# A fused attention and gated-MLP kernel: the row sums of one weight matrix split over two stages, output weights loaded later, transposes interleaved

## The chip, the cores and the metric

The kernel runs on one core of a Trainium2 chip. The metric is the time of one execution on the device in microseconds (us), lower is better. A core has TensorE (matmuls), VectorE, ScalarE and GpSimd, SyncE (SP) that mostly issues transfers, and 16 DMA engines that move data between device memory (DRAM) and the on-chip SBUF. Each engine works through its own instructions in order and waits on semaphores for others.

## The reference

Inputs are bf16; S = 2048 tokens, D = 1024, 32 heads of 32, FH = 1792.

```python
# A: sliding dilated attention; window of 8, dilation 2
qkv = layernorm(x) @ wqkv            # per token and head: softmax over k at s, s-2, ..., s-14
h = x + attn @ wo
# B: gated MLP with a spatial (token by token) mix
z = gelu(layernorm(h) @ w_in)        # [S, 2*FH]
z1, z2 = z[:, :FH], layernorm(z[:, FH:])
g = w_sp @ z2 + b_sp[:, None]        # w_sp is [S, S]
out = h + (z1 * g) @ w_out
```

## The kernel before, in words

Tokens are cut into four chunks of 512 (`NCH`), each of four tiles of 128 (`TPC`). Three stages follow each other.

**Attention and projections, chunk by chunk.** `qkv` multiplies the normed chunk with the weights; ScalarE copies each result out of PSUM (L461 into the tiles of chunk 0, L466 into a staging tile that SP stores to `qkv_d`). `attention` works on VectorE: products of q and k (L513), sums, then the scores go through TensorE (L543), a maximum, ScalarE's exp (L564) and a reciprocal. Half of the weights reach all partitions by way of DRAM: SP stores `att_d` and loads it back into `AB` (L592), and VectorE's products with v for the last four window places (L629) wait for it. GpSimd issues two accumulating DMAs for the first four. The result `oT` goes to `head` (L700: times wo, plus the residual, a layernorm, and an SP transpose into `hnT`; the last chunk has one transpose for each tile). Then `b_z2` (L777) and `b_z1` (L831) multiply with w_in; the gelu is ScalarE's; `z2` gets its second layernorm (the `l3` values, L808 on VectorE for the last chunk) and both are stored to DRAM. In the last chunk ScalarE issues these stores itself.

The order on TensorE, ScalarE, VectorE and GpSimd is written out by a planner (`Order`): each step has an engine, an assumed cost in us, its predecessors and a priority, and the planner runs through the steps in assumed time. Steps of kind `DMA` with a cost stand for transfers or for plain delays. The engines' instructions are then issued in that order; on the chip only semaphores decide the times. From `close_` on SP's order is by hand too.

**Row sums of w_sp.** The weight matrix w_sp is scaled per row by a power of two, so that its products fit fp16. For that `wsp_sums` loads its 16 row tiles (`wn`, 512 KB each, from ScalarE's DMA queue, four buffers) and ScalarE adds up absolute values in two halves of each (L859). `row_scales` turns the 16 columns into scales on VectorE; they are turned on TensorE, stored (`rs_d`) and loaded on all partitions (`rows`). In the planner the loads start at 45 us and follow every 8 us.

**The spatial stage.** w_sp is loaded transposed by SP (`load_raw`: chunks 0 and 1 as rawa and rawb before the stage, 2 and 3 within it), multiplied by `rows` (`scale_raw`, L897), and combined into three forms (`t_forms`). The product with z2 is done by seven half-size products in place of eight for each block (L1011), for each of two pairs of chunks (`pr`) and seven pairs of feature tiles (`i`; `n = 7 pr + i`). For one n, TensorE runs k1, k4, k3, k2 (8 matmuls each), then second products into k1, k4 and k3 (8 each). Before those ScalarE must have copied k1 to p1, k4 to p7 and k3 to p5 (L1047, L1049, L1051). VectorE forms the sums of z2 for the next n (`z_form`, tiles `zs`), then combines the results with p1, p7, p5 (L1065 to L1075), and GpSimd helps (L1056 to L1071). z2f and z1c are loaded two and one n ahead by SP.

**The output projection** follows each pair of chunks: eight row tiles (`il`), 28 matmuls each (L1092), with VectorE's residual (L1095) and, in the first pair, the scaling and the forms of chunks 2 and 3. Its weights `wout_a` and `wout_b` are loaded by GpSimd's queue as soon as the planner's part is written out.

Of the kernel before, what the change touches and what calls it, by code (L numbers as in the profile page):

```python
# [24 lines left out]
CH = 512  # L25
NCH = S // CH
TPC = CH // P
KT = D // P
DLO = 8
HALO = 16  # L30
# [10 lines left out]
L2DVE = (0, 0, 2)  # L41
PIECES = ((0, 0), (0, 4), (1, 0), (1, 4))
LNPRIO = (0, 2.0, 2.5, 2.8)
WSP_FROM, WSP_EVERY = 45.0, 8.0
HK = S // P // 2
LAST_COLS = ((0, 512), (512, 896), (896, 1024))

# [83 lines left out]
def kernel(  # L131
# [260 lines left out]
    def dma_op(us, fn, deps, lat=0.1, free=None):  # L392
        return add("DMA", us, fn, deps, lat=lat, free=free)
# [453 lines left out]

    def wsp_sums():
        tl = {}
        for i in range(NT):  # L850
            def ld(i=i):
                tl[i] = l1.tile([P, S], BF16, name="wn", tag="x4k", bufs=4)
                A.dma_start(tl[i][:], B_w_sp[i * P:(i + 1) * P, :])
            gate = add("DMA", WSP_FROM + WSP_EVERY * i, lambda: None)
            l_ = dma_op(4.0, ld, [gate, wabs_ops[i - 4] if i >= 4 else G["normed", 2]])
            for hf in range(2):
                def ab(i=i, hf=hf):
                    h_ = tl[i][:, hf * D:(hf + 1) * D]
                    A.activation(h_, h_, ACTF.Abs, accum_out=wabs[:, i, hf:hf + 1])  # L859
                a_ = add("ACT", 1.22, ab, [l_], prio=5.8)  # L860
            wabs_ops.append(a_)

    def row_scales():
        V.tensor_tensor(wlim[:], wabs[:, :, 0], wabs[:, :, 1], op=ALU.add)
        V.tensor_scalar(wlim[:], wlim[:], 2.0 ** -40, 2.0 ** 60, op0=ALU.max, op1=ALU.min)
        V.tensor_scalar(wexp[:], wlim[:].bitcast(I32), 0x7F800000, None, op0=ALU.bitwise_and)
        V.tensor_scalar(rsc[:], wexp[:], -1.0, float(266 << 23), op0=ALU.mult, op1=ALU.add)
        V.tensor_scalar(rinv[:], wexp[:], float(-(12 << 23)), None, op0=ALU.add)
        V.tensor_copy(rsc16[:], rsc[:].bitcast(FP32))

    def rows_turned():
        wt_["ps"] = ps_acc.tile([P, 2, 2 * CH], BF16, name="rps", tag="acc")
        T.transpose(wt_["ps"][0:NT, 0, 0:P], rsc16[:], ident[:])

    def rows_out():
        A.copy(rscT[0:NT, :], wt_["ps"][0:NT, 0, 0:P])
        dma(rs_d[:], rscT[0:NT, :])

    def rows_in():
        wt_["rows"] = zpools["z"].tile([P, S], BF16, name="rows")  # L880
        dma(wt_["rows"][:], rs_d[:].rearrange("i p -> (i p)").unsqueeze(0).to_broadcast([P, S]))

    def bias_rows(pr, pool, tag, bufs):
        cols = slice(2 * pr * CH, (2 * pr + 2) * CH)
# [30 lines left out]
    def load_z2f(n, hf):  # L915
        if hf == 0:
            z2f[n] = zpools["z"].tile([P, NT, 2 * P], BF16, name="z2f", tag="z2f", bufs=2)
        i = n % (NF // 2)
        dma(z2f[n][:, hf * HK:(hf + 1) * HK, :], z2_view[:, hf * HK:(hf + 1) * HK, 2 * i * P:(2 * i + 2) * P])
# [44 lines left out]
        zpools["z"] = ctx.enter_context(tc.tile_pool(name="zpool", bufs=1, side="right"))  # L964

    head(NCH - 1)
    rs_ = add("DVE", 1.0, row_scales, [G["avdone", NCH - 1]] + wabs_ops, prio=2.8)
    rt_ = add("PE", 0.1, rows_turned, [rs_], prio=0.5, take="acc", lat=0.2)
    ro_ = add("ACT", 0.3, rows_out, [rt_], prio=1.0, free="acc")
    rl_ = dma_op(4.0, rows_in, [(ro_, 2.5), G["close"]])  # L970
    b_z2(NCH - 1)
    b_z1(NCH - 1)
    r0_ = dma_op(9.0, lambda: load_raw(0), [G["hnT", NCH - 1]])
    r1_ = dma_op(9.0, lambda: load_raw(1), [r0_])
    prev = []
    for c, r_ in ((0, r0_), (1, r1_)):
# [5 lines left out]
    z_ld = {}  # L982
    for n in range(2):
        for hf in range(2):
            z_ld[n, hf] = dma_op(4.0, lambda n=n, hf=hf: load_z2f(n, hf), [r1_] + [G["z2st", 2 * hf + c, il] for c in range(2) for il in range(TPC)])
    prev = None
    for m in (3, 1, 2, 4):
        prev = add("DVE", 0.7, lambda m=m: z_form(0, m), [z_ld[0, 0]] + ([z_ld[0, 1]] if m != 3 else []) + ([prev] if prev else []), prio=3.0)
    o_.run()
    wout_a = wtile([P, 8, D], "wout_a", "wA")  # L990
    wout_b = wtile([P, NF - 8, D], "wout_b", "wA")
    wout_view = B_w_out.rearrange("(f p) n -> p f n", p=P)
    dma_w(wout_a[:], wout_view[:, 0:8, :])
    dma_w(wout_b[:], wout_view[:, 8:NF, :])
    t2.close()
    bph_stack.close()
    ps_stack.close()
# [29 lines left out]
    for pr in range(NCH // 2):  # L1027
# [5 lines left out]
        for i in range(NQ):  # L1033
            n = pr * NQ + i
            z = z2f[n]
            a11, a12, a22 = z[:, 0:HK, 0:P], z[:, HK:NT, 0:P], z[:, HK:NT, P:2 * P]
            p1, p7, p5, u = f32("p1"), f32("p7"), f32("p5"), f32("u2")
            if n == 0:
                load_z1c(0)
            if n + 1 < 2 * NQ:  # L1040
                load_z1c(n + 1)
            if i == 0:
                zg = p2.tile([P, NF, 2 * CH], BF16, name="zg", tag="zg", bufs=1)
            z1c = z1cs[n]
            k1, k4, k3, k2 = bank(), bank(), bank(), bank()
            times(k1, a11, b11, True)
            A.copy(p1[:], k1[:])  # L1047
            times(k4, zs[n, 3], t3, True)
            A.copy(p7[:], k4[:])  # L1049
            times(k3, zs[n, 1], t1_, True)  # L1050
            A.copy(p5[:], k3[:])  # L1051
            times(k2, zs[n, 2], t2_, True)
            times(k1, a12, b21, False)
            times(k4, a22, t4_, False)
            times(k3, zs[n, 4], b22, False)
            nc.gpsimd.tensor_tensor(p7[:], p7[:], p5[:], op=ALU.add)  # L1056
            if pr == 0 and i < TPC:
                load_raw(2, i, i + 1)
            if i + 1 < NQ:
                for m in (3, 1, 2, 4):  # L1060
                    z_form(n + 1, m)
            if n + 2 < 2 * NQ:
                for hf in range(2):
                    load_z2f(n + 2, hf)
            V.tensor_tensor(u[:], k2[:], p1[:], op=ALU.add)  # L1065
            nc.gpsimd.tensor_tensor(p1[:], u[:], bt1, op=ALU.add)
            nc.gpsimd.tensor_tensor(u[:], u[:], bt2, op=ALU.add)
            z11, z12 = zg[:, 2 * i, 0:CH], zg[:, 2 * i, CH:2 * CH]
            z21, z22 = zg[:, 2 * i + 1, 0:CH], zg[:, 2 * i + 1, CH:2 * CH]
            V.tensor_tensor(z11, k1[:], bt1, op=ALU.add)  # L1070
            nc.gpsimd.tensor_tensor(z22, p7[:], u[:], op=ALU.add)  # L1071
            V.tensor_tensor(z21, k4[:], p1[:], op=ALU.add)
            V.tensor_tensor(zg[:, 2 * i + 1, :], zg[:, 2 * i + 1, :], z1c[:, 1, :], op=ALU.mult)
            V.tensor_tensor(z12, k3[:], u[:], op=ALU.add)
            V.tensor_tensor(zg[:, 2 * i, :], zg[:, 2 * i, :], z1c[:, 0, :], op=ALU.mult)  # L1075
            if pr == 0 and i > TPC:
                scale_raw(2, (i - TPC - 1) * HK)
            if i == NQ - 2:
                for il in range(3):
                    load_hr(2 * pr * TPC + il)  # L1080
        for il in range(2 * TPC):
# [28 lines left out]
                    finish_(lo, hi, acc)  # L1110
                    (A.dma_start if n % 2 else dma)(out2d[t * P:(t + 1) * P, lo:hi], hr[:, lo:hi])
            if pr == 0:
                if il == 3:
                    scale_raw(3, 0)
                    scale_raw(3, HK)
                elif il == 4:
# [41 lines left out]
```

## Time and profile before

| | |
|---|---|
| median of 3 runs | 742.01 us (741.72 to 742.41) |
| the profiled execution | 742.02 us, its span 740.0 us |
| mean granted TensorE clock | 0.979 |
| busy: TensorE, VectorE, ScalarE, GpSimd | 95%, 68%, 37%, 16% |
| DMA | 133 MB, 180 GB/s in the mean |
| chain that ended last | TensorE 78%, DMA 10%, VectorE 7% |

The span is the time from the first to the last instruction of the profiled execution; around it lie 2.0 us. In the profile PE is TensorE, PEld its weight loads, DVE VectorE, ACT ScalarE, POOL GpSimd, SP SyncE; `ACTq` and `SPq` are the queues' own instructions, such as the issue of a DMA. L1011 is a line of the kernel. A tile's name is followed by `<-` and what it is made from. The 40 slices are 18.5 us each; a digit is the busy share in tenths.

### The profile page before, as it was taken

How to read it: one execution, taken by the hardware profiler on the slowest of the kernel's cores; microseconds unless marked ns; L12 is line 12 of the kernel's file. 1: busy time of each engine (PE TensorE's matmuls, PEld its weight loads, DVE VectorE, ACT ScalarE, POOL GpSimd, SP SyncE). 2: the span in 40 equal slices, each digit the busy share in tenths (PEclk: the TensorE clock that was granted, in tenths of full speed). 3: DMA queues.
4: the chain of work that ended last, by engine and by line, in shares of the span. 5: the costliest groups of instructions: out<-in, count | busy, mean ns of one | idle time of the engine just before them, and what ended most of it. 6: DMA issues, size and time to landing. Idle time of an engine off the chain costs nothing.

```text
span 740.0 us, 8761 instructions
## 1 busy us (share of the span) xinstructions
PE 701.0 (95%) x3399; PEld 360.9 (49%) x3426; DVE 504.7 (68%) x593; ACT 274.7 (37%) x387; POOL 115.2 (16%) x107
## 2 busy tenths in 40 slices
PE   9999984999956999999999999699999999999998
PEld 7766652466622544544444454244444444444444
DVE  6899829897478979999796345565553775554322
ACT  4445643485331778674774562111110000101000
POOL 0100100001110111010030011044350005343100
PEclk9999998899988999999999999899999999999999
DMA  9965797569968056945175898686649323543031
GB/s 334 295 191 171 232 236 250 130 185 320 234 233 314 29 156 203 263 161 154 48 162 200 196 246 310 192 217 171 163 136 208 105 86 98 158 111 118 29 93 49
DMA packets 145337, 133.04 MB, mean 180 GB/s; under 512 B 68688, under 2 KB 117232, under 8 KB 145168
## 3 DMA queue, kind: packets, MB, share of 16 engines
q1 hardware_dynamic: 132592, 88.93, 42.4%
q0 software_dynamic: 7488, 31.13, 15.1%
q10 hardware_dynamic: 5216, 12.42, 5.0%
q8 instruction: 27, 0.44, 0.3%
q14 instruction: 14, 0.11, 0.0%
HBM read 75.24 MB, written 33.10 MB: 146 GB/s over the span
## 4 chain that ended last, share of the span: by engine, by line
PE 78%; DMA 10%; DVE 7%; ACT 1%; issue 1%; SPq 1%; POOL 0%; ACTq 0%; DVEq 0%; POOLq 0%
PE bank L1011 22%; PE bank L1092 13%; PE acc L777 12%; PE acc L455 11%; PE acc L831 10%; PE acc L700 8%; DMA AB<-att_d 3%; DVE av_b L637 2%; DMA att_d<-attn 2%; PE acc L301 2%; DVE av_p L629 2%; DMA z_d<-u 2%; DMA wn<-in_B_w_sp_dram 1%; DMA z_d<-z1s 1%; SPq L592 1%
## 5 line engine op out<-in xcount | busy, mean ns | idle before, releaser
L831 PE MATMUL acc<-hnT,win 128*128 128x512 bf16 x448 | 98.0, 379 | 0.0
L777 PE MATMUL acc<-win,hnT 128*128 128x512 bf16 (+1 forms) x501 | 97.4, 352 | 0.6
L700 PE MATMUL acc<-wo_sb,av_oT 128*128 128x512 bf16 x250 | 59.6, 397 | 16.5 <-DVE av_oT L637 16.0
L513 DVE TENSOR_TENSOR prod<-qT,kT 128x4096 bf16<-128x4096 bf16 x32 | 72.7, 2283 | 1.7 <-ACT kT L461 1.3
L777 PEld LDWEIGHTS <-hnT 128*128 128x128 bf16 x512 | 49.9, 98 | 47.5 <-issue 0.7
L1092 PEld LDWEIGHTS <-zg 128*128 128x128 bf16 x462 | 44.7, 98 | 52.4
L1011 PEld LDWEIGHTS <-zs 128*128 128x128 f16 x448 | 44.0, 98 | 53.6 <-issue 1.4
L831 PEld LDWEIGHTS <-win 128*128 128x128 bf16 x448 | 43.7, 98 | 52.6 <-issue 0.7
L1047 ACT COPY p<-bank 128x512 f32<-128x512 f32 x14 | 8.2, 585 | 161.0 <-PE bank L1011 150.5
L455 PE MATMUL acc<-xnT,wv 128*128 128x512 bf16 x256 | 58.0, 387 | 7.9 <-ACT stg L466 7.9
L1011 PE MATMUL bank<-rawa,z2f 128*128 128x512 f16 x224 | 54.6, 388 | 6.3 <-ACT z1s L837 4.5
L1095 DVE SCALAR_TENSOR_TENSOR hr<-bank,rinv_w,hr 128x512 bf16<-128x512 f32 (+2 forms) x33 | 22.9, 731 | 53.7 <-PE bank L1092 53.6
L455 PE MATMUL acc<-xnT,wk 128*128 128x512 bf16 x256 | 56.7, 379 | 2.8 <-ACT stg L466 2.8
L1092 PE MATMUL bank<-wout_a,zg 128*128 128x512 bf16 (+2 forms) x258 | 57.9, 372 | 0.3
L1011 PEld LDWEIGHTS <-z2f 128*128 128x128 bf16 x336 | 33.2, 99 | 47.2 <-issue 8.5
L1011 PE MATMUL bank<-rawb,zs 128*128 128x512 f16 x224 | 53.4, 382 | 0.0
L466 ACT CAST stg<-acc 128x1024 bf16<-128x1024 f32 x36 | 35.8, 1008 | 43.2 <-DMA qkv_d<-stg 20.8
L1011 PE MATMUL bank<-form,zs 128*128 128x512 f16 x224 | 50.7, 379 | 0.0
L455 PEld LDWEIGHTS <-wv 128*128 128x128 bf16 x256 | 36.8, 144 | 28.3 <-issue 10.4
L700 PEld LDWEIGHTS <-av_oT 128*128 128x128 bf16 x256 | 25.8, 102 | 49.4 <-DVE av_oT L637 16.8
L455 PEld LDWEIGHTS <-wk 128*128 128x128 bf16 x256 | 36.5, 143 | 22.0 <-issue 4.0
L1092 PE MATMUL bank<-wout_b,zg 128*128 128x512 bf16 (+2 forms) x194 | 44.2, 372 | 0.2
(174 smaller groups left out, 938.4 us busy)
## 6 DMA issues: line engine op xcount, KB each, us to landing
z2f<-z_d SPq DMA_DIRECT2D x28, 512.0 KB, 4.9
qkv_d<-stg SPq DMA_DIRECT2D x36, 256.0 KB, 4.2
wn<-in_B_w_sp_dram ACTq DMA_DIRECT2D x16, 512.0 KB, 4.5
z1c<-z_d SPq DMA_DIRECT2D x14, 512.0 KB, 4.0
z_d<-z1s SPq DMA_DIRECT2D x21, 256.0 KB, 2.4
z_d<-u SPq DMA_DIRECT2D x12, 448.0 KB, 2.6
av_y<-av_z POOLq DMA_DIRECT2D x4, 1024.0 KB, 9.2
av_oT<-av_zz POOLq DMA_DIRECT2D x4, 1024.0 KB, 12.8
```

The lines of the kernel that those rows point to most:

```text
L301: T.matmul(dst.rearrange("p (a b) -> p a b", b=P), wqs[:, kt, dl, :], xnT[0][:, lo:hi, kt, :], start=start, stop=stop)
L455: T.matmul(G[key][:, j, :].rearrange("p (a b) -> p a b", a=TPC), wv[:, kt, dl, :], xnT[c][:, :, kt, :], start=(kt == 0), stop=(kt == KT - 1))
L466: A.copy(stg[:], G[key][:])
L513: V.tensor_tensor(st["prod"][:], qT[:], kT[:, :, o:o + CH], op=ALU.mult)
L629: V.tensor_tensor(av[key][:].rearrange("p d (q s) -> p d q s", q=4), vs.rearrange("p d (q s) -> p d q s", q=4), abb, op=ALU.mult)
L637: V.tensor_tensor(av[to][:], av[to][:], av[key][:], op=ALU.add)
L700: T.matmul(st["acc", il][:, nh, :], oTs[c][:, dl, il * P:(il + 1) * P], wo_sb[:, dl, nh * CH:(nh + 1) * CH], start=(dl == 0), stop=(dl == ...
L777: T.matmul(accf[:, n0:n1], hnTs[c][:, il, kt, :], wins[hf][:, kt, n0:n1], start=(kt == 0), stop=(kt == KT - 1))
L831: T.matmul(G["accy", c, fp][:, j, :].rearrange("p (a b) -> p a b", a=TPC), wt[:, kt, f0 * P:(f0 + 1) * P], hnTs[c][:, :, kt, :], start=(kt ...
L1011: T.matmul(dst[:], wts[:, k, :], mov[:, k, :], start=(first and k == 0), stop=(k == HK - 1), skip_group_check=not first)
L1092: T.matmul(outs, zg[:, f, il * P:(il + 1) * P], wt[:, f0, lo:hi], start=(f == 0), stop=(f == NF - 1))
L1095: V.scalar_tensor_tensor(hr[:, lo:hi], acc[:, 0:hi - lo], rv[:, t:t + 1], hr[:, lo:hi], op0=ALU.mult, op1=ALU.add)
```

## The change

The 16 row sums are split by pairs of chunks (`TPP` = 8 tiles each). The first eight stay in `wsp_sums`, with loads planned from 40 us, every 4.5 us; the sums of the seventh and eighth are held in the plan until 90 us. The other eight go into the spatial stage of the first pair, two tiles in each of i = 2 to 5, from a pool `p2` with two buffers, written out behind the copies p1, p7 and p5 of that i; at i = 5 `row_scales` for them follows on VectorE ahead of `z_form` of the next n, and the scales go out through GpSimd's queue with an access pattern that turns them, and back in on SP. The loads of rawa for chunk 2 move from i = 0 to 3 to i = 2 to 5, and its scaling from i = 5 and 6 to the projection's il = 2. The loads of `wout_a` and `wout_b` move from ahead of the spatial stage to n = 1. The load of rawa for chunk 0, one transpose before, is cut in three (a quarter, a quarter, a half), and the quarters are issued on SP ahead of the third and the fourth `hnT`. On VectorE both scalings of rawb and form 0 now stand ahead of the `l3` values of the last chunk, and the bias rows and most of `z_form(0)` behind the forms. TensorE's order is unchanged, apart from the smaller transpose of the scales.

```diff
--- before.py
+++ after.py
@@ -25,6 +25,7 @@
 CH = 512
 NCH = S // CH
 TPC = CH // P
+TPP = 2 * TPC
 KT = D // P
 DLO = 8
 HALO = 16
@@ -41,7 +42,8 @@
 L2DVE = (0, 0, 2)
 PIECES = ((0, 0), (0, 4), (1, 0), (1, 4))
 LNPRIO = (0, 2.0, 2.5, 2.8)
-WSP_FROM, WSP_EVERY = 45.0, 8.0
+WSP_FROM, WSP_EVERY = 40.0, 4.5
+WSP_HELD = (6, 90.0)
 HK = S // P // 2
 LAST_COLS = ((0, 512), (512, 896), (896, 1024))
 
@@ -847,38 +849,49 @@
 
     def wsp_sums():
         tl = {}
-        for i in range(NT):
+        for i in range(TPP):
             def ld(i=i):
-                tl[i] = l1.tile([P, S], BF16, name="wn", tag="x4k", bufs=4)
-                A.dma_start(tl[i][:], B_w_sp[i * P:(i + 1) * P, :])
+                load_wn(i, l1, "x4k", 4)
             gate = add("DMA", WSP_FROM + WSP_EVERY * i, lambda: None)
-            l_ = dma_op(4.0, ld, [gate, wabs_ops[i - 4] if i >= 4 else G["normed", 2]])
+            l_ = dma_op(8.0, ld, [gate, wabs_ops[i - 4] if i >= 4 else G["normed", 2]])
+            if i >= WSP_HELD[0]:
+                l_ = add("DMA", WSP_HELD[1], lambda: None)
             for hf in range(2):
-                def ab(i=i, hf=hf):
-                    h_ = tl[i][:, hf * D:(hf + 1) * D]
-                    A.activation(h_, h_, ACTF.Abs, accum_out=wabs[:, i, hf:hf + 1])
-                a_ = add("ACT", 1.22, ab, [l_], prio=5.8)
+                a_ = add("ACT", 1.22, lambda i=i, hf=hf: row_sum(i, hf), [l_], prio=5.8)
             wabs_ops.append(a_)
 
-    def row_scales():
-        V.tensor_tensor(wlim[:], wabs[:, :, 0], wabs[:, :, 1], op=ALU.add)
-        V.tensor_scalar(wlim[:], wlim[:], 2.0 ** -40, 2.0 ** 60, op0=ALU.max, op1=ALU.min)
-        V.tensor_scalar(wexp[:], wlim[:].bitcast(I32), 0x7F800000, None, op0=ALU.bitwise_and)
-        V.tensor_scalar(rsc[:], wexp[:], -1.0, float(266 << 23), op0=ALU.mult, op1=ALU.add)
-        V.tensor_scalar(rinv[:], wexp[:], float(-(12 << 23)), None, op0=ALU.add)
-        V.tensor_copy(rsc16[:], rsc[:].bitcast(FP32))
+    wn = {}
+
+    def load_wn(i, pool, tag, bufs):
+        wn[i] = pool.tile([P, S], BF16, name="wn", tag=tag, bufs=bufs)
+        A.dma_start(wn[i][:], B_w_sp[i * P:(i + 1) * P, :])
+
+    def row_sum(i, hf):
+        h_ = wn[i][:, hf * D:(hf + 1) * D]
+        A.activation(h_, h_, ACTF.Abs, accum_out=wabs[:, i, hf:hf + 1])
+
+    def row_scales(pr):
+        n = slice(pr * TPP, (pr + 1) * TPP)
+        V.tensor_tensor(wlim[:, n], wabs[:, n, 0], wabs[:, n, 1], op=ALU.add)
+        V.tensor_scalar(wlim[:, n], wlim[:, n], 2.0 ** -40, 2.0 ** 60, op0=ALU.max, op1=ALU.min)
+        V.tensor_scalar(wexp[:, n], wlim[:, n].bitcast(I32), 0x7F800000, None, op0=ALU.bitwise_and)
+        V.tensor_scalar(rsc[:, n], wexp[:, n], -1.0, float(266 << 23), op0=ALU.mult, op1=ALU.add)
+        V.tensor_scalar(rinv[:, n], wexp[:, n], float(-(12 << 23)), None, op0=ALU.add)
+        V.tensor_copy(rsc16[:, n], rsc[:, n].bitcast(FP32))
 
     def rows_turned():
         wt_["ps"] = ps_acc.tile([P, 2, 2 * CH], BF16, name="rps", tag="acc")
-        T.transpose(wt_["ps"][0:NT, 0, 0:P], rsc16[:], ident[:])
+        T.transpose(wt_["ps"][0:TPP, 0, 0:P], rsc16[:, 0:TPP], ident[:])
 
     def rows_out():
-        A.copy(rscT[0:NT, :], wt_["ps"][0:NT, 0, 0:P])
-        dma(rs_d[:], rscT[0:NT, :])
-
-    def rows_in():
-        wt_["rows"] = zpools["z"].tile([P, S], BF16, name="rows")
-        dma(wt_["rows"][:], rs_d[:].rearrange("i p -> (i p)").unsqueeze(0).to_broadcast([P, S]))
+        A.copy(rscT[0:TPP, :], wt_["ps"][0:TPP, 0, 0:P])
+        dma(rs_d[0:TPP, :], rscT[0:TPP, :])
+
+    def rows_in(pr):
+        if pr == 0:
+            wt_["rows"] = zpools["z"].tile([P, S], BF16, name="rows")
+        dma(wt_["rows"][:, 2 * pr * CH:(2 * pr + 2) * CH],
+            rs_d[pr * TPP:(pr + 1) * TPP, :].rearrange("i p -> (i p)").unsqueeze(0).to_broadcast([P, 2 * CH]))
 
     def bias_rows(pr, pool, tag, bufs):
         cols = slice(2 * pr * CH, (2 * pr + 2) * CH)
@@ -964,13 +977,15 @@
         zpools["z"] = ctx.enter_context(tc.tile_pool(name="zpool", bufs=1, side="right"))
 
     head(NCH - 1)
-    rs_ = add("DVE", 1.0, row_scales, [G["avdone", NCH - 1]] + wabs_ops, prio=2.8)
+    rs_ = add("DVE", 1.0, lambda: row_scales(0), [G["avdone", NCH - 1]] + wabs_ops, prio=2.8)
     rt_ = add("PE", 0.1, rows_turned, [rs_], prio=0.5, take="acc", lat=0.2)
     ro_ = add("ACT", 0.3, rows_out, [rt_], prio=1.0, free="acc")
-    rl_ = dma_op(4.0, rows_in, [(ro_, 2.5), G["close"]])
+    rl_ = dma_op(4.0, lambda: rows_in(0), [(ro_, 2.5), G["close"]])
     b_z2(NCH - 1)
     b_z1(NCH - 1)
-    r0_ = dma_op(9.0, lambda: load_raw(0), [G["hnT", NCH - 1]])
+    r0_ = dma_op(2.2, lambda: load_raw(0, 0, 1), [G["close"], rl_.deps[0], (G["hnT", NCH - 1, 1], 0.0 - 3.9)])
+    r0_ = dma_op(2.2, lambda: load_raw(0, 1, 2), [r0_, (G["hnT", NCH - 1, 2], 0.0 - 3.9)])
+    r0_ = dma_op(5.5, lambda: load_raw(0, 2, TPC), [r0_, (G["hnT", NCH - 1, 3], 0.0 - 3.9)])
     r1_ = dma_op(9.0, lambda: load_raw(1), [r0_])
     prev = []
     for c, r_ in ((0, r0_), (1, r1_)):
@@ -982,16 +997,13 @@
     z_ld = {}
     for n in range(2):
         for hf in range(2):
-            z_ld[n, hf] = dma_op(4.0, lambda n=n, hf=hf: load_z2f(n, hf), [r1_] + [G["z2st", 2 * hf + c, il] for c in range(2) for il in range(TPC)])
-    prev = None
+            z_ld[n, hf] = dma_op(6.0, lambda n=n, hf=hf: load_z2f(n, hf), [r1_] + [G["z2st", 2 * hf + c, il] for c in range(2) for il in range(TPC)])
     for m in (3, 1, 2, 4):
-        prev = add("DVE", 0.7, lambda m=m: z_form(0, m), [z_ld[0, 0]] + ([z_ld[0, 1]] if m != 3 else []) + ([prev] if prev else []), prio=3.0)
+        prev = [add("DVE", 0.7, lambda m=m: z_form(0, m), [z_ld[0, 0]] + ([z_ld[0, 1]] if m != 3 else []) + prev, prio=3.65)]
     o_.run()
     wout_a = wtile([P, 8, D], "wout_a", "wA")
     wout_b = wtile([P, NF - 8, D], "wout_b", "wA")
     wout_view = B_w_out.rearrange("(f p) n -> p f n", p=P)
-    dma_w(wout_a[:], wout_view[:, 0:8, :])
-    dma_w(wout_b[:], wout_view[:, 8:NF, :])
     t2.close()
     bph_stack.close()
     ps_stack.close()
@@ -1054,8 +1066,19 @@
             times(k4, a22, t4_, False)
             times(k3, zs[n, 4], b22, False)
             nc.gpsimd.tensor_tensor(p7[:], p7[:], p5[:], op=ALU.add)
-            if pr == 0 and i < TPC:
-                load_raw(2, i, i + 1)
+            if n == 1:
+                dma_w(wout_a[:], wout_view[:, 0:8, :])
+                dma_w(wout_b[:], wout_view[:, 8:NF, :])
+            if pr == 0 and 2 <= i < 2 + TPC:
+                load_raw(2, i - 2, i - 1)
+                for t in (TPP + 2 * i - 4, TPP + 2 * i - 3):
+                    load_wn(t, p2, "wn", 2)
+                    row_sum(t, 0)
+                    row_sum(t, 1)
+                if i == 1 + TPC:
+                    row_scales(1)
+                    dma_w(rs_d[TPP:NT, :].rearrange("i p -> p i"), rsc16[:, TPP:NT])
+                    rows_in(1)
             if i + 1 < NQ:
                 for m in (3, 1, 2, 4):
                     z_form(n + 1, m)
@@ -1073,8 +1096,6 @@
             V.tensor_tensor(zg[:, 2 * i + 1, :], zg[:, 2 * i + 1, :], z1c[:, 1, :], op=ALU.mult)
             V.tensor_tensor(z12, k3[:], u[:], op=ALU.add)
             V.tensor_tensor(zg[:, 2 * i, :], zg[:, 2 * i, :], z1c[:, 0, :], op=ALU.mult)
-            if pr == 0 and i > TPC:
-                scale_raw(2, (i - TPC - 1) * HK)
             if i == NQ - 2:
                 for il in range(3):
                     load_hr(2 * pr * TPC + il)
@@ -1110,7 +1131,10 @@
                     finish_(lo, hi, acc)
                     (A.dma_start if n % 2 else dma)(out2d[t * P:(t + 1) * P, lo:hi], hr[:, lo:hi])
             if pr == 0:
-                if il == 3:
+                if il == 2:
+                    scale_raw(2, 0)
+                    scale_raw(2, HK)
+                elif il == 3:
                     scale_raw(3, 0)
                     scale_raw(3, HK)
                 elif il == 4:
```

## The prediction

> **What bounds the kernel now.** I read the page first, then TensorE's waits, then the chain of waits in order of time, then the timeline around the three places where TensorE stands still, and last the rows of the tiles that the change moves.
>
> The page gives the engines and the 40 slices:
>
> ```profile
> PE 701.0 (95%) x3399; PEld 360.9 (49%) x3426; DVE 504.7 (68%) x593; ACT 274.7 (37%) x387; POOL 115.2 (16%) x107
> PE   9999984999956999999999999699999999999998
> DMA  9965797569968056945175898686649323543031
> ```
>
> TensorE is the bound. Its 39 us of idle time sit in slices 6, 11 to 12 and 25: the attention of chunk 0, that of chunk 1, and the switch to the spatial stage. Only there, or by a new stall, can time move. TensorE's waits name what it waits for (us in total, times, longest):
>
> ```profile
> PE acc L700 <- DVE av_oT L637: 16.0, 2, 10.3
> PE acc L455 <- ACT stg L466: 10.7, 2, 7.9
> PE bank L1011 <- ACT z1s L837: 4.5, 1, 4.5
> PE bank L1011 <- ACT p L1047: 1.8, 1, 1.8
> ```
>
> The chain (start, us, what) shows what stands behind them: transfers.
>
> ```profile
> 84.43 9.88 DMA att_d<-attn
> 97.63 10.86 DMA AB<-att_d
> ...
> 446.71 11.12 DMA z_d<-u
> 457.91 7.46 DMA z_d<-z1s
> 465.39 4.50 DMA z2f<-z_d
> ```
>
> The spatial stage itself has no gap: 56 matmuls of 0.2163 us, 12.1 us for each n.
>
> **Attention: row sums of 8 tiles leave it.** Before, 16 loads of 512 KB run from 44 to 190 us. In the changed program eight remain, all issued by about 73 us, between copies that ScalarE makes anyway (one of 1.01 us each 3.45 us; a tile's two sums add 2.2 us, so 3.2 of 3.45 us are used: cost 0, and 2 us if a load comes late there). The load issued at 84.09 took 10.1 us to land, right beside att_d, and the one at 94.33 took 7.6 us, beside AB. Slices 4 and 5 move 232 to 236 GB/s, so 512 KB less is up to 2.2 us for each of the two transfers, 0 if they wait for the 1 MB kT load and the two accumulating DMAs instead. I take 3.5 of 4.4 us for chunk 0: VectorE waits for AB at 108.6 and TensorE for VectorE, so all of it reaches TensorE. Chunk 1 has one such load (181.13, 8.9 us to land) before its att_d: I take 2. The exp of chunk 1 also comes 1 us earlier, but att_d is queued on SP behind a store whose matmuls end at 182.04, so that gains nothing. Sum: **5.5 us less** (2 to 8; the range also takes in the 2 us of a late load).
>
> **The switch: output weights leave, transposes go between the hnT's.** wout_a and wout_b (3.5 MB, issued at 445 and 446) took 13.2 and 18.7 us to land and share the DMA engines with z_d<-u and z_d<-z1s. Without them I price those stores by their medians on SP, 2.6 and 2.4 us, and add 1.5. TensorE ends z1 at 462.4 and reaches the second half of n=0 at 478.0: 15.6 us, of which 32 matmuls are 6.9. Left after the change is ScalarE's last z1s (1.02 us and its wait), 1.3 us. So 15.6 - 6.9 - 1.3 = **7.4 us less**, if nothing else is late. What could be:
> - The transposes. SP issued two hnT in 4.1, rawa in 8.3 and rawb in 8.8 us, from 416.0 to 437.4, without a pause. The new order puts a quarter of rawa ahead of hnT 2 and of hnT 3. Quarters cost 2.5 to 4.3 us of SP in the spatial stage. hnT 2 is then issued at 418.4 to 420.1 and is needed at 426.0 (413.9 + 2 x 6.05), landing in some 5.3: between 2 us spare and nothing. rawb lands at 438.5 to 443 (before, about 440).
> - VectorE now has both scalings of rawb and form 0 (3 x 2.28) ahead of the l3 moments, which ended at 441.4 before. They move to 446 to 450, GpSimd's 3.1 and the four norms' 3.2 us follow, the stores of u are issued by 454 to 457 and the second z2f half, the bias rows and the first zs of that half follow by 465 to 468. k3 wants that zs at 467.1, because k1 and k4 use the first half only: between 2 us spare and 1 late.
> - ScalarE waits for those norms before it issues the stores, with the third z1s behind it. Three accumulators of 3.45 us cover it until 455.4; the late end costs 2.4 us.
> So 4 to 7.4 us; I keep 7.3.
>
> **The spatial stage: eight tiles on ScalarE.** In i = 2 to 5 ScalarE gets, behind the copies p1, p7, p5: load, two sums, load, two sums. The question is whether the second load waits until the sums before it are done. The timeline has the like:
>
> ```profile
> 172.57 1.06 ACT L859 ACTIVATE wn<-wn 128x1024 bf16<-128x1024 bf16 x1 [3.67 <-DMA wn<-in_B_w_sp_dram]
> ...
> 172.71 0.33 ACTq L853 DMA_DIRECT2D wn<-in_B_w_sp_dram  x1
> ...
> 174.67 0.99 ACT L466 CAST stg<-acc 128x1024 bf16<-128x1024 f32 x1
> 175.56 0.20 ACT L558 ACTIVATE texp<-eps_t 128x1 f32<-128x1 f32 x1
> ```
>
> In the program's order that load stands behind the second sum, the stg copy and texp, and it was issued 0.14 us after the wait ended, 2.9 us ahead of texp. So ScalarE's queue blocks at a wait, but not behind work that is ready. By that row a load is issued some 0.2 us after the previous tile landed. [...]
>
> Times within n, from TensorE's start T: p5's copy can start at T+5.4 and the first load goes out with it; with A and B the landing times, the second tile's sums end at T+5.45+A+0.2+B+2.2 = T+7.85+A+B. TensorE wants p1 of the next n at 12.1+6.9. So nothing stalls until A+B passes 10.6. For A and B the trace has this:
>
> ```profile
> DMA to landing us min/median/max: 3.4/4.5/10.1
> ```
>
> Eight of those 16 landed in 3.4 to 4.3; those started behind a 1 MB transfer took 7.6 to 10.1. Here A meets the tail of a transposed quarter of raw 2 (issued some 2.7 us ahead) and B the two z2f loads (4.9 each when alone). I take A+B = 10.4, between 7.2 (clear) and 16 (both behind). Hence no stall in n = 4 and 5, and about 1.5 us at n = 3, where wout (now issued by GpSimd at n=1) still runs (0 to 4.4).
>
> The cost comes at the end. At i=5 row_scales stands on VectorE ahead of z_form(6) and waits for the last sums: T+7.85+10.4, then 1.0 us (six operations from 397.33 to 398.33) and 0.7 us for the first zs. k4 of n=6 wants that zs at T+12.1+1.73. Stall: A+B-4.1 = 6.3 us. Behind VectorE's wait stand all of z_form(6) and the epilogue of n=5; the projection reaches its last zg 5.2 us after the stage, which just holds. Sum: **8 us more** (3 at A+B = 7.2; 25 at 16, where each n is paced by the loads).
>
> Without a price of their own: wout's issue holds GpSimd for 2.3 us at n=1, hidden because its 4.8 us fit in 12.1; the 2-byte scattered store of rsc16 and rows_in hold SP, with z2f(7) and three hr loads behind, needed first when banks run out, 24 us into the projection; the scalings of raw 2 move to il=2, 4.6 + 1.5 us of VectorE in 6.05 of TensorE, ahead of banks by three pairs.
>
> **Sum.** 742.02 us is the profiled execution (span 740.0, 2.0 around it), as good as the median 742.01. 742.0 - 5.5 - 7.3 + 8 = 737.2; I say **737**.
>
> **Rivals.**
> 1. The loads are clear: A+B = 7.2, 3 us of stall, attention gives 8: 742 - 8 - 7.3 + 3 = 730. For it: the eight clear landings, and z1c lands in a median of 4.0 in this stage. Against: three queues share the engines there. Chance 0.18.
> 2. Slower: ScalarE paces the stage. If A+B is above 10.6, p1 is late in n = 3 to 6 and the price is 4(A+B) - 39 us. It decides from A+B = 13, where 13 us eat both gains. At 16: 742 - 12.8 + 25 = 754. If a load did wait for the sums ahead of it, k4 of n=6 would come 6.0 + 8 x (5.2 + 2.2) + 3 copies' 4.7 + 1.8 = 71.7 us after n=2's start in place of 50.1: 22 us, 751. For it: 7.6 to 10.1 us behind other transfers; against: the row at 172.71. Chance 0.25.
> 3. The change does not do what it says: AB waits for the accumulating DMAs and not for the loads (2 us), the late rawb costs the switch half (4 us), the stall stays 8: 744. Chance 0.15.
> 4. The scattered store blocks SP. rsc16 goes out in 1,024 elements of 2 bytes. A packet took 51 ns in the mean (62.5% of 16 engines x 740 us over 145,337 packets): 3.3 us over 16 engines, 52 us if one engine does them all. The slack is 27 us (11 to the stage's end, 24 of banks, less 8 for rows and hr), so 25 are too many: 762. For it only that no row shows such a store. Chance 0.02. [...]
>
> **The numbers.** Forecast 0.40. A measurement of this kernel tells 0.2% (1.5 us) from no change. Faster takes nearly all of the forecast, rival 1, and a little of rival 3: 0.59. Same 0.10, slower 0.31 (rivals 2 and 4, most of 3). The range 729 to 750 leaves out the ends of rivals 1 and 2. The forecast's own range is 733 to 740.
>
> **What would show it.** Right: no wait of L1011 for z1s over 1.5 us and the z_d<-u piece under 5 us; TensorE waits once for zs at n=6, about 6 us; the waits for av_oT at L700 fall from 16 to about 10. Wrong: TensorE waits for p L1047 in each of n = 3 to 6 (rival 2); an att_d and AB piece as long as before (rival 3); L777 waiting for hnT. If the wn landings of the spatial stage are above 6.5 us in the mean, the forecast falls.

## The result and the profile after

| | before | after |
|---|---|---|
| median | 742.56 us (739.14 to 744.44, 20 runs) | 736.21 us (728.14 to 744.50, 20 runs) |
| the profiled execution | 742.02 us, span 740.0 | 735.56 us, span 733.8 |
| mean granted clock | 0.979 | 0.984 |

The ratio of comparable runs is 0.9902, with a 95% interval of 0.9881 to 0.9922: faster by about 7 us. The ratios leave out executions that are slower as a whole, at a lower granted clock (the profiled ones of wout_late and after_again below, at 0.655 and 0.557) or over 1.5% above the fastest of their kernel, so where a kernel's time varies they can lie below the ratio of the medians. The forecast was 737. The time is right; two of its terms are not, and that they nearly cancel is luck.

From here on the lines are those of the changed kernel: L700 has become L702, L1011 L1023, L1047 L1059, L853 L867, L859 L871, L892 L905, L1025 L1037 (L893 now loads the rows). TensorE's 40 slices after (18.3 us each, counted from 0):

```profile
PE   8999997999679999999999999999799989999998
```

The holes of attention (slice 6, slices 10 and 11) are shorter, that of the switch (slice 25 before) is gone, and two new ones have come: slice 28, inside the first half of the spatial stage, and slice 32, at the start of the second half. TensorE's waits after (us in total, times, longest):

```profile
PE acc L702 <- DVE av_oT L639: 9.0, 2, 5.0
PE bank L1023 <- DVE zs L940: 7.3, 2, 5.1
PE acc L457 <- ACT stg L468: 5.6, 1, 5.6
...
PE bank L1023 <- ACT z1s L839: 1.1, 1, 1.1
```

The wait for av_oT fell from 16.0 to 9.0, that for stg from 10.7 to 5.6, that for z1s from 4.5 to 1.1. New is zs, 7.3 us in two waits; one was forecast. In the chain of waits the same two transfers of chunk 0 stand (9.88 and 10.86 before), and the stores of z_d are gone from it:

```profile
84.37 6.52 DMA att_d<-attn
...
93.73 6.36 DMA AB<-att_d
```

Where TensorE's matmuls start gives the balance (us; each piece is read between the same two groups of matmuls in both profiles):

| piece | forecast | measured | from |
|---|---|---|---|
| attention of chunk 0, to the head matmuls (L702) | -3.5 | -8.4 | 129.44 to 121.05 |
| attention of chunk 1, to its head matmuls | -2.0 | -3.9 | 228.15 to 215.85, less the 8.4 |
| head 1 to the end of z1 | 0 | +0.3 | 234.3 to 234.6 |
| end of z1 to the second half of n=0 | -7.3 | -7.6 | 15.6 to 8.0 |
| from there to the end of the first spatial half | +8 | +9.1 | 77.7 to 86.8 |
| from there to the last matmul, and the tail | 0 | +4.3 | 181.5 to 185.5 |
| sum | -4.8 | -6.2 | span 740.0 to 733.8 |

The new stalls stand in TensorE's timeline like this (start, us, instruction, idle before and releaser):

```profile
496.60 1.89 PE L1023 MATMUL bank<-rawa,z2f 128*128 128x512 f16 x8 [1.70 <-ACT p L1059]
...
532.98 3.59 PE L1023 MATMUL bank<-rawb,zs 128*128 128x512 f16 x8 [5.13 <-DVE zs L940]
536.36 3.83 PE L1023 MATMUL bank<-form,zs 128*128 128x512 f16 x16
...
597.57 3.00 PE L1023 MATMUL bank<-rawb,zs 128*128 128x512 f16 x8 [2.12 <-DVE zs L940]
```

The first two are the forecast's n=3 (1.5 expected) and n=6 (6.3 expected). VectorE's timeline names the cause of the second, as the prediction had it: row_scales waited for the last sums, with z_form(6) behind it.

```profile
531.34 0.17 DVE L875 TENSOR_TENSOR wlim<-wabs 128x8 f32<-128x8 f32 x1 [12.44 <-ACT wn L871]
```

The third, at n=7, was not forecast.

### The profile page after: what moved, and what is told of

The parts are those of the page before. It is cut to its first block, busy times and chain, and to the rows that moved or that the text cites. A ratio compares the mean times of both kernels' runs of the same rounds, so it can differ in the third digit from the quotient of the medians.

```text
span 733.8 us, 8797 instructions
## 1 busy us (share of the span) xinstructions
PE 703.2 (96%) x3426; PEld 360.8 (49%) x3426; DVE 506.1 (69%) x599; ACT 275.6 (38%) x387; POOL 117.0 (16%) x108
## 4 chain that ended last, share of the span: by engine, by line
PE 72%; DMA 10%; DVE 9%; SPq 4%; issue 2%; ACT 1%; POOL 0%; ACTq 0%; DVEq 0%; POOLq 0%
PE bank L1023 20%; PE acc L457 12%; PE acc L833 11%; PE acc L779 9%; PE bank L1113 9%; PE acc L702 8%; DMA wn<-in_B_w_sp_dram 3%; DVE av_b L639 3%; SPq L905 2%; DMA AB<-att_d 2%; DMA rawb<-in_B_w_sp_dram 2%; PE acc L303 2%; DMA att_d<-attn 2%; DVE av_p L631 2%; DVE rawb L910 1%
## 5 line engine op out<-in xcount | busy, mean ns | idle before, releaser
L833 PE MATMUL acc<-hnT,win 128*128 128x512 bf16 x448 | 98.2, 379 | 0.6 <-ACT z1s L839 0.6
L1023 PEld LDWEIGHTS <-zs 128*128 128x128 f16 x448 | 44.5, 100 | 63.3 <-DVE zs L940 8.2
L833 PEld LDWEIGHTS <-win 128*128 128x128 bf16 x448 | 43.7, 98 | 53.3 <-issue 1.5
L702 PE MATMUL acc<-wo_sb,av_oT 128*128 128x512 bf16 x256 | 59.1, 393 | 9.0 <-DVE av_oT L639 9.0
L1023 PE MATMUL bank<-rawb,zs 128*128 128x512 f16 x224 | 55.7, 394 | 7.3 <-DVE zs L940 7.3
L1023 PE MATMUL bank<-rawa,z2f 128*128 128x512 f16 x224 | 52.9, 379 | 2.8 <-ACT p L1059 1.7
L1059 ACT COPY p<-bank 128x512 f32<-128x512 f32 x14 | 8.1, 579 | 123.8 <-PE bank L1023 120.4
L1023 PEld LDWEIGHTS <-z2f 128*128 128x128 bf16 x336 | 32.8, 98 | 42.9 <-issue 3.4
L1023 PE MATMUL bank<-form,zs 128*128 128x512 f16 x224 | 51.5, 383 | 0.0
L702 PEld LDWEIGHTS <-av_oT 128*128 128x128 bf16 x256 | 25.6, 101 | 41.6 <-DVE av_oT L639 9.8
```

What stands on the lines that cost most here:

```text
L702: T.matmul(st["acc", il][:, nh, :], oTs[c][:, dl, il * P:(il + 1) * P], wo_sb[:, dl, nh * CH:(nh + 1) * CH], start=(dl == 0), stop=(dl == ...
L833: T.matmul(G["accy", c, fp][:, j, :].rearrange("p (a b) -> p a b", a=TPC), wt[:, kt, f0 * P:(f0 + 1) * P], hnTs[c][:, :, kt, :], start=(kt ...
L1023: T.matmul(dst[:], wts[:, k, :], mov[:, k, :], start=(first and k == 0), stop=(k == HK - 1), skip_group_check=not first)
```

## The experiments

Twelve kernels were run, each timed in five rounds against the kernel before. One number serves for the second part of the program: from the second half of n=0 to the last matmul it is 259.2 us before and 272.2 after. This stretch lies behind the attention, whose time varies between executions of the same code (last section). Where the medians below come from six runs that spread over 7 to 15 us, the waits and this stretch carry the argument.

| run | median us | ratio to before, 95% interval |
|---|---|---|
| no_tiles_5_6 | 738.95 | 0.9956 (0.9935 to 0.9977) |
| no_tile_14 | 740.55 | 0.9991 (0.9973 to 1.0008) |
| no_tile_15 | 734.70 | 0.9914 (0.9881 to 0.9946) |
| wout_late | 734.97 | 0.9909 (0.9893 to 0.9924) |
| transposes_between | 746.99 | 1.0067 (1.0043 to 1.0090) |
| after_again (the changed kernel) | 736.31 | 0.9927 (0.9899 to 0.9956) |
| no_late_sums | 723.45 | 0.9693 (0.9645 to 0.9740) |
| scales_later | 732.38 | 0.9803 (0.9754 to 0.9853) |
| rows_by_scalar | 731.88 | 0.9870 (0.9827 to 0.9913) |
| later_and_scalar | 730.79 | 0.9838 (0.9799 to 0.9877) |
| store_turned | 724.57 | 0.9736 (0.9690 to 0.9781) |
| turned_ahead | 723.28 | 0.9718 (0.9681 to 0.9754) |

### Which loads made the attention shorter

Three kernels are the one before without single tiles; their row sums are a constant instead.

```
                 if i not in (5, 6):          # no_tiles_5_6; (14,) and (15,) in the others
                     A.dma_start(tl[i][:], B_w_sp[i * P:(i + 1) * P, :])
```

> The kernel before, without the loads and row sums of tiles 5 and 6 (their sums are a constant; 2 of 16 tiles are left out), all other instructions in the same order. These are the loads issued at 84 and 94 us, beside att_d and AB of chunk 0. Theory (the attention's gain in chunk 0 comes from the DMA traffic of these two loads): att_d takes 6 to 7 us in place of 9.9, AB is there some 8 us earlier, the first head starts near 121 in place of 129.4, and the time is 6 to 9 us below before. Rival (the gain comes from ScalarE's freed time and the new plan as a whole): head starts within 2 us of before, time 0 to 2 us below.

> The kernel before, without load and sums of tile 14 alone (its sum is a constant). Its load is issued at 172.7 and ScalarE waits for it until 180.9 with a stg copy behind, whose store stands on SP ahead of att_d of chunk 1. Theory (chunk 1 gains by ScalarE's queue no longer blocked): that stg comes about 3 us earlier, att_d of chunk 1 too, and the time is 2.5 to 3.5 us below before. Rival (the prediction's reading: the store is paced by TensorE, and chunk 1 gains by less traffic beside att_d): 0 to 0.5 us.

> The kernel before, without load and sums of tile 15 alone (its sum is a constant). Its load is issued at 181.1, 2.3 us ahead of att_d of chunk 1. The prediction's price: 2 us below before, since att_d shares the DMA engines with it. Theory now: att_d and AB of chunk 1 are as long as before (8.2 and some 15 us), within 0.7 us of before.

Tiles 5 and 6, the loads at 84.09 and 94.33, are worth 3.3 us by the ratio. In the profile att_d landed in 7.91 us in place of 9.88, AB in 9.45 in place of 10.86, and head 0 starts at 126.36 in place of 129.44. That is near the forecast's 3.5, and half of the 6 to 9 us that the theory of this run expected. Without tile 14 ScalarE was free earlier, and att_d of chunk 1 was issued at 180.02 in place of 183.42, but it then landed in 9.45 us in place of 8.19, with the 2 MB load of win issued at 178.74, 1.28 us ahead of it (4.25 before): nothing measurable gained, and not the theory's 2.5 to 3.5. Tile 15, the load at 181.13, missed its expectation by far: 6.4 us by the ratio. The chain without it, in chunk 1:

```profile
183.53 5.45 DMA att_d<-attn
...
190.99 7.38 DMA AB<-att_d
```

Before, the same two were

```profile
183.42 8.19 DMA att_d<-attn
...
195.35 11.88 DMA AB<-att_d
```

One 512 KB load beside two small transfers that wait for each other costs them 7.2 us here, of the 8.6 by which the piece of chunk 1 is shorter, not the 2 that I took for it. The sums of the tile left ScalarE too, so the 6.4 us are for load and sums together.

### The output weights and the transposes, each by itself

```
-    dma_w(wout_a[:], wout_view[:, 0:8, :])     # wout_late: these two lines go to n == 1,
-    dma_w(wout_b[:], wout_view[:, 8:NF, :])    # as in the changed kernel
```

> The kernel before, with only the loads of the output weights moved to n=1. Theory (these loads made the switch's stores late): the z_d<-u piece falls from 11 to under 5 us, TensorE's z1 to second half of n=0 from 15.6 to 8 to 9 us, and the time is 6 to 7.5 us below before. Rival (the transposes between the hnT's and the new order on VectorE are what shortens the switch): 0 to 2 us below.

6.7 us by the ratio: the output weights alone gain nearly all that the forecast gave to the whole step. The pieces that the expectation names can't be compared, since the profile ran at a clock of 0.655. The other half of it:

```
-    r0_ = dma_op(9.0, lambda: load_raw(0), [G["hnT", NCH - 1]])
+    r0_ = dma_op(2.2, lambda: load_raw(0, 0, 1), [G["close"], rl_.deps[0], (G["hnT", NCH - 1, 1], 0.0 - 3.9)])
+    r0_ = dma_op(2.2, lambda: load_raw(0, 1, 2), [r0_, (G["hnT", NCH - 1, 2], 0.0 - 3.9)])
+    r0_ = dma_op(5.5, lambda: load_raw(0, 2, TPC), [r0_, (G["hnT", NCH - 1, 3], 0.0 - 3.9)])
```

> The kernel before with only raw 0's transpose split and its first quarters put between the hnT's. Theory (the switch waits for stores beside the output weights, not for transposes): no change, 741 to 743. Rival (the transposes shorten the switch): 738.

Neither: 5 us slower. From the new dependencies the planner also made another order on VectorE, so the run holds both. Its waits of TensorE:

```profile
PE bank L1013 <- ACT z1s L837: 4.8, 1, 4.8
PE acc L831 <- ACT z1s L837: 3.3, 1, 3.3
PE bank L1013 <- DVE zs L927: 2.9, 1, 2.9
```

The second line is the late z1s, the third the late zs of the second half, that the prediction weighed: the l3 moments run after both scalings of rawb (GpSimd's part at 451.67, before 441.54), the norms of u at 454.62, the store of u goes out at 457.86 beside the output weights, and z1s stands behind it. In the changed kernel the output weights are not there, the same chain ends in time, and L833 waits 0.6 us. So the transposes, with that order, cost 5 us where the output weights are early. With those late, at most the 0.6 us of that wait can be laid to them, and the 7.6 us of the whole switch are hardly more than the 6.7 without them.

### The stalls of the spatial stage

no_late_sums leaves out the eight loads and sixteen sums of the spatial stage; the second half's scales are made from the first half's sums.

```
-                for t in (TPP + 2 * i - 4, TPP + 2 * i - 3):
-                    load_wn(t, p2, "wn", 2)
-                    row_sum(t, 0)
-                    row_sum(t, 1)
```

> The changed kernel without the eight loads and sixteen sums of the spatial stage (the second half's scales are made from the first half's sums, by one copy more); row_scales(1), the scattered store and rows_in(1) stay at i=5. Theory (the loads make the stalls at n=3 and n=6, and the late store the one at n=7): all three go, since the store is issued some 27 us ahead of the stage's end and lands 14 us later: 723. Rival (the store in itself costs 4 us wherever it stands, by holding SP's queue): 727, with a wait for zs or z2f at n=6 or 7.

723.45: 12.8 us under the changed kernel, and the stretch of 259.2 us is back (259.2). The spatial stage and what follows it cost 13 us, then, where the forecast had 8. Against the kernel before, attention and switch together are worth 18.6 us by the medians and 12.1 in the profile, where the forecast had 12.8; the runs lie between 715 and 730 us, so the median's closeness to the expected 723 says little. One detail of the expectation was wrong: the scattered store went out 16 us, not 27, ahead of the stage's end (the first matmul of the projection).

What makes the wait at n=7? SP's timeline after, from the moment it is free again (the columns are start, time of the issues, queue, line):

```profile
546.62 0.34 SPq L893 DMA_DIRECT2D rows<-rs_d  x1
...
548.12 5.12 SPq L1037 DMA_DIRECT2D hr<-h_d  x3
...
559.32 8.68 SPq L905 DMA_TRANSPOSE rawb<-in_B_w_sp_dram  x2
...
571.32 5.19 SPq L905 DMA_TRANSPOSE rawb<-in_B_w_sp_dram  x2
```

Before, the second pair of these transposes stood at

```profile
566.39 6.22 SPq L892 DMA_TRANSPOSE rawb<-in_B_w_sp_dram  x2
```

The scattered store was issued at 532.6 and took 14.0 us to land; SP stood at the load of the rows until then. Behind it stand the transposes of rawb for the second half. Before, the two pairs went out 0.7 and 10.7 us after the stage's end (555.67 before, 545.20 after), now 14.1 and 26.1 us. VectorE waits for rawb until 578.80, and its forms and the first zs of n=7 follow:

```profile
578.80 4.49 DVE L910 TENSOR_TENSOR rawb<-rawb,rows 128x4096 f16<-128x4096 bf16 x2 [8.03 <-DMA rawb<-in_B_w_sp_dram]
```

Three kernels take this apart:

```
+            if pr == 0 and i == NQ - 1:      # scales_later: all three lines from i == 1 + TPC to here
+                row_scales(1)
+                dma_w(rs_d[TPP:NT, :].rearrange("i p -> p i"), rsc16[:, TPP:NT])
+                rows_in(1)                   # rows_by_scalar: only this, as rows_in(1, A.dma_start)
                                              # later_and_scalar: both
```

> The changed kernel once more, as the base for the three that follow: about 736 us against 742 before. TensorE's wait for zs at n=6 about 5 us, its wait for zs at n=7 about 2 us, the scattered store of rsc16 lands some 14 us after its issue. If one of these three is missing here, the reading of the first profile as a mechanism falls.

> The changed kernel with row_scales(1), the scattered store and rows_in(1) moved from i=5 to i=6, behind z_form(6) and the epilogue on VectorE. Theory (VectorE's wait for the last sums makes the stall at n=6, the late rows make the one at n=7): the wait for zs at n=6 and the slow matmuls behind it go (7 us), the store is issued at about the same time on the clock, so relative to the stage's end it comes 7 us later, and the wait at n=7 grows by 5 to 7 us: 735 to 737, no change against the changed kernel. Rival (the store is off the path, n=7 waits for something else): 729.

> The changed kernel with only the load of the rows (rows_in(1)) taken from SP's queue to ScalarE's, behind the copies of n=6, so that SP does not wait for the scattered store. Theory (the hold of SP for 13 us makes the wait at n=7): the wait for zs at n=7 (2.1) and the slow matmuls behind it (1.9) go, the stall at n=6 stays at 5 us: 732. Rival (the rows themselves are late, not what is queued behind them): 736, wait at n=7 as before.

> Both edits: row_scales(1) and the store at i=6, and the rows loaded by ScalarE's queue. Theory: both stalls go, 7 + 4 us under the changed kernel: 725 (723 to 728). Rival (the rows are late by then, since the store is issued when it was and takes 14 us): the wait at n=7 stays, 729 to 732.

The changed kernel's median came again (736.31). Of the three signs that its expectation names only one could be seen again, the store, which took 14.2 us to land: at a clock of 0.557 TensorE waits at neither n=6 nor n=7. rows_by_scalar came out as the theory said: the wait at n=7 is gone, that at n=6 stays (5.1), 731.88 for 732; the stretch is 269.1 us. scales_later lost the stall at n=6 as it should, but the wait at n=7 grew from 2.1 to 3.9 only and not by 5 to 7, so its 732.38 missed the 735 to 737 (stretch 266.8): at i=6 the three hr loads stand ahead of the rows on SP and no longer behind, so the transposes came only 1.6 to 1.9 us later against the stage's end. later_and_scalar missed its theory's 725: its wait at n=7 stayed at 2.3, the rival's line and the rival's time (730.79 against its 729 to 732; stretch 265.4). SP's timeline there shows why, though SP waits for no row:

```profile
533.54 8.46 SPq L1037 DMA_DIRECT2D hr<-h_d  x1
542.10 15.47 SPq L905 DMA_TRANSPOSE rawb<-in_B_w_sp_dram  x2
```

The chain of waits names the transpose that VectorE's scaling of rawb, at 567.83, waited for:

```profile
562.93 4.78 DMA rawb<-in_B_w_sp_dram
```

The rows, as the rival says, were late too: they landed at 557.9 and the scaling of rawa began then, but it was done at 562.4, and rawb came later. One hr load and the first two quarters took 24 us of SP; before it was 1.06 and 6.69. The scattered store was in flight from 531.0 to 547.9. So it does not only hold who waits for it: SP's other issues were slow while it ran. It was not the bandwidth that was short. In the 14.0 us of the store in the changed kernel the 16 DMA engines were busy 3% of the time and moved 1 GB/s; here, from 533 to 542, it was 28% and 31 GB/s. How the store slows SP, no run shows. The next kernel takes the store itself away, and keeps the later row_scales:

```
+        if pr == 0:                                   # ahead of the projections
+            rps = psq.tile([P, 2 * CH], BF16, name="rps", tag="bank", bufs=8)
+            T.transpose(rps[0:TPP, 0:P], rsc16[:, TPP:NT], ident[:])
+            A.copy(rscT[0:TPP, :], rps[0:TPP, 0:P])
+            A.dma_start(rs_d[TPP:NT, :], rscT[0:TPP, :])
+            rows_in(1, A.dma_start)
```

> The changed kernel with row_scales(1) at i=6, and the scattered store replaced: the row scales are transposed on TensorE at the end of the stage, copied and stored as whole rows (2 KB in 8 rows), and the rows are loaded, both on ScalarE's queue. Theory (the scattered store, while it is in flight, slows SP's transposes, and that makes the wait at n=7): the store lands in 3 to 4 us, the two transposes of rawb ahead of the first projections take about 7 us on SP as in the kernel before, no wait for zs at n=7; from the second half of n=0 to the end 260 us (before 258.7, changed kernel 271.7): 725. Rival (raw 3's transposes are late for another reason, the three hr loads and z2f ahead of them): 728 to 730, wait at n=7 stays at 2 us or more.

The same 2 KB in whole rows were issued at 544.66, and the load of the rows behind them at 549.31, 4.7 us later, where the scattered store took 14.0 to 16.9 us in four profiles. SP is free at once:

```profile
543.54 1.32 SPq L1037 DMA_DIRECT2D hr<-h_d  x1
544.96 6.56 SPq L905 DMA_TRANSPOSE rawb<-in_B_w_sp_dram  x2
...
557.40 4.43 SPq L905 DMA_TRANSPOSE rawb<-in_B_w_sp_dram  x2
```

No wait at n=7, 261.1 us for the stretch (expected 260, which counts to the start of the last matmul group and so 0.5 us less), 724.57 us (expected 725). The eight profiles together give a clear line: TensorE waits at n=7 where the second pair of rawb goes out late after the stage's end.

| kernel | second pair, us after the stage's end | TensorE's wait at n=7 | stretch |
|---|---|---|---|
| before | 10.7 | 0 | 259.2 |
| turned_ahead | 12.8 | 0 | 261.1 |
| store_turned | 13.1 | 0 | 261.1 |
| rows_by_scalar | 17.4 | 0 | 269.1 |
| no_late_sums | 21.9 | 0 | 259.2 |
| after | 26.1 | 2.1 | 272.2 |
| later_and_scalar | 26.5 | 2.3 | 265.4 |
| scales_later | 27.8 | 3.9 | 266.8 |

The last run adds a third buffer, three loads at n=1 and then one behind each tile's sums:

```
+            if pr == 0 and i == 1:
+                for t in range(TPP, TPP + 3):
+                    load_wn(t, p2, "wn", 3)
...
+                    if t + 3 < NT:
+                        load_wn(t + 3, p2, "wn", 3)
```

> The same, and the loads of wn run ahead: three buffers in place of two, three loads at n=1 and one behind each tile's sums, so that ScalarE's sums find their tile landed. Theory: the wait for p at n=3 (1.7 us) and the small ones at n=5 go too: 1 to 3 us under the run with only the store replaced, 723 to 724, and from the second half of n=0 to the end 258.7 us as before the change. Rival (the three early loads collide with wout at n=1 and come late at n=2 and 3): p waits at n=2 or 3 by 2 to 6 us, 727.

The wait for p at n=3 (1.4 in store_turned) went, and 1.3 us of waits for z2f and zs came in its place at the same n, right behind the output weights (wout_b landed at 486.1, TensorE waits at 486.75 and 491.40): the stretch is 261.1 us again and not back at that of before, as expected. So the third buffer gained nothing, and 723.28 us are not told apart from store_turned's 724.57. By the medians both beat the changed kernel by 12 to 13 us and the kernel before by 17 to 19; by the stretch they beat the changed kernel by 11.

## Why the prediction was right, and where it was not

**Attention: right for chunk 0, wrong for chunk 1.** Forecast 5.5 less (2 to 8), in this profile 12.3. In chunk 0 the 3.5 was what no_tiles_5_6 measured (3.3), by the mechanism that the prediction named; the other 5 us of this profile are told in the last section. In chunk 1 the forecast's 2 us were to come from shorter transfers beside one load less, and this step failed. In the changed kernel the transfers of chunk 1 are as long as before:

```profile
171.43 8.19 DMA att_d<-attn
...
183.23 11.71 DMA AB<-att_d
```

The 3.9 us gained there come from an earlier start: counted from head 0, att_d goes out 3.6 us earlier. The prediction said that att_d "is queued on SP behind a store whose matmuls end at 182.04, so that gains nothing". The timeline of before has it otherwise; ScalarE waited for a tile, with the stg copy of that store behind it:

```profile
180.89 1.06 ACT L859 ACTIVATE wn<-wn 128x1024 bf16<-128x1024 bf16 x1 [3.19 <-DMA wn<-in_B_w_sp_dram]
...
181.95 0.99 ACT L466 CAST stg<-acc 128x1024 bf16<-128x1024 f32 x1
```

In the changed kernel stg follows its matmuls at once. Yet the price of the load itself, "I take 2", was too small: it is 6.4 us by no_tile_15. The changed kernel does not get it. There the load of win is issued 1.27 us ahead of att_d, in no_tile_15 4.74 us, and in no_tile_14, with 1.28, att_d was no shorter either (9.45 us). That win takes the place of the load is a reading of these rows; no run moves win alone.

**The switch: right.** 7.3 forecast, 7.6 measured, nearly all of it the output weights (6.7 alone). The two risks that the prediction weighed for the transposes, TensorE waiting for z1s in z1 and for zs in the second half, are what transposes_between shows, with 3.3 and 2.9 us beside early output weights; in the changed kernel 0.6 us of the first is left.

**The spatial stage: right in place, nearly in size.** 8 forecast, 9.1 measured: 1.70 for 1.5 at n=3, 5.13 for 6.3 at n=6, since the last two loads took about 9.7 us together and not 10.4. (The forecast's A+B-4.1 should be A+B-4.3 by its own terms, 7.85 and 1.7 against 13.83.) The loads ran ahead of the queue as the row at 172.71 had said (ScalarE's timeline after):

```profile
487.98 1.06 ACT L871 ACTIVATE wn<-wn 128x1024 bf16<-128x1024 bf16 x1 [6.24 <-DMA wn<-in_B_w_sp_dram]
487.99 0.35 ACTq L867 DMA_DIRECT2D wn<-in_B_w_sp_dram  x1
```

The eight wn landings of the spatial stage are 3.4, 5.0 and 6.8 us (least, median, longest). The first pair, behind the output weights, took about 12.7 us together, just under the 13 from which rival 2 decides; the other three pairs took 9 to 10, so ScalarE did not pace the stage. What the sum lacked is the 1.9 us of slow matmuls behind the wait at n=6 (3.59 + 3.83 us in place of 1.89 + 3.62).

**The store: the other step that failed.** "The 2-byte scattered store of rsc16 and rows_in hold SP, with z2f(7) and three hr loads behind, needed first when banks run out" was priced at nothing; it cost 4.0 us, 2.1 of waiting and 1.9 of slower matmuls behind the wait. The list of what stands behind was short: the four transposes of rawb were left out, and with them the scalings, the forms and the zs of n=7. Rival 4 had the mechanism, but put the point from which it decides at 27 us for the store. The store took 14.0 us and that was enough, because the table above sets the limit by the transposes, somewhere between 22 and 26 us after the stage's end. The factor between the scattered store and a turned tile in whole rows is 3 to 3.6 here (14.0 to 16.9 against 4.7 us).

So the forecast was 6.8 us short on the gains of attention and 5.4 us short on the cost of the spatial stage and what follows. Their difference is small, and the time came out 0.8 us from the median. That is luck. Over the seven profiles with the changed attention head 1 starts 5.4 to 19.7 us earlier than before, in three of them by 5.4 to 7.1, close to the forecast's 5.5; with that timing the changed kernel would take 741 to 742 us (an estimate: the profiled 735.6, with 5.2 to 6.9 us less gain; four of its twenty runs took 740.8 to 744.5).

## What to carry to other kernels

When a step with a DMA is moved, list everything that the queue issues behind it until the work that needs it, transposes for the next stage too, and not only the loads that stand next. A load beside small transfers on the path cost more here than its own time on the wires (7.2 us for one of 512 KB that would need 2.2 at the 234 GB/s of slice 10 before, an estimate), so look first for what is issued just ahead of them. The two kilobytes of scales were cheaper turned on TensorE and stored in rows than stored element by element: that, with the scales taken behind the next forms, brought 11 to 12 us.

## What was not expected of the hardware

**The same attention code falls into three timings.** Seven profiles have the changed attention, and head 0 starts at about 126.4 (three times), 121 (twice) or 115.8 (twice). The timelines differ in how far the 1 MB load of kT is issued ahead of att_d; first rows_by_scalar, then scales_later:

```profile
83.26 0.89 POOL L488 DMA_DIRECT2D kT<-qkv_d  x1 [10.59 <-issue]
...
84.15 0.42 SPq L592 DMA_DIRECT2D att_d<-attn  x1
```

```profile
83.83 0.89 POOL L488 DMA_DIRECT2D kT<-qkv_d  x1 [11.02 <-ACT stg L468]
...
84.30 0.42 SPq L592 DMA_DIRECT2D att_d<-attn  x1
```

att_d landed in 7.9 and 2.6 us. With kT 0.47 us ahead (two profiles) it is 2.6, with 0.65 us (turned_ahead) 6.4, with 0.82 to 0.89 (three) 7.6 to 8.0, and with 1.09, in the profile after, 6.5. So differences of 0.2 us in the issue of a load go with 5 us at the end of attention. Where kT is clearly ahead the order is not strict, no run moves kT alone, and what sets the timing from run to run stays open. It is a likely reason why the runs of the changed kernel spread over 16 us (728 to 744) and those of before over 5, and why one profile's attention can't be taken for the median's.

**TensorE was slow behind some waits.** The granted clock by windows of the profile after (window, its length, PE busy and matmuls, clock, DMA share, GB/s):

```profile
533.00:537.00 4.00, 4.00 (x10) 0.53 0.10 1
537.00:541.00 4.00, 4.00 (x20) 1.00 0.01 2
```

Behind the 5.13 us of waiting 10 matmuls fit in 4 us, at a granted clock of 0.53, afterwards 20. A shorter wait did it as well: behind 2.12 us, at n=7 after, 8 matmuls took 3.00 us in place of 1.89 (granted clock 0.65 from 597 to 601), while behind 2.34 in later_and_scalar they took 1.90. What decides between the two, no run shows. The stall of 5 us at n=6 cost 7.
